# Turning the normalised x of one batch by DMA transpose instead of on TensorE, in a fused linear-attention and MLP kernel

## The chip, the cores and the metric

The kernel runs on one core of a Trainium2 chip. The metric is the time of one execution on the device, in microseconds; lower is better. A time is given as the median of several executions, and one more execution was recorded with a profile.

## The reference, cut to what matters

There are 8 batches, 8 heads, 576 positions and 64 numbers per head. Attention has no softmax: one 64x64 matrix per head is formed from k and v, and q is multiplied by it.

```
kv  = einsum('bhsd,bhse->bhde', k, v)
o   = einsum('bhsd,bhde->bhse', q, kv)
x   = o / sqrt(mean(o*o over the 64 of a head) + 1e-6) * g_norm   # heads joined: [8, 576, 512]
xn  = (x - mean(x)) / sqrt(var(x) + 1e-6) * g_ln                  # over the 512
out = x + relu(xn @ w_ch1) @ w_ch2                                # 512 -> 2048 -> 512
```

## The kernel before, in words

**Tiles.** The 576 positions of a batch are four tiles of 128 rows and a remainder of 64. Remainders of two batches make one tile, so a ninth block, "rem", has four tiles. Every tile of rows passes through these steps (class `Tile`):

- `o` (L259): four small matmuls on TensorE of the turned q (`qt`) with the batch's `kv_pack`, into PSUM `o_ps`.
- `sq` (L265, ScalarE), `red` (L286, VectorE), `root` (L296, ScalarE), `inv` (L303), `y` (L291), `x` (L310) and `xc` (L320), all on VectorE: the two normalisations, without the last division. `xc` ends in a bf16 tile [128 rows, 512].
- `var` (L328, ScalarE): the row variance, used only at the very end of the tile.
- `turn`: `xc` must be laid with its 512 along the partitions before the first big matmul. With `turn(True)` TensorE transposes the four 128x128 blocks into the PSUM tile `tp` (L336) and ScalarE copies `tp` into the columns of this tile in `xT_blk` (L338). With `turn(False)` one DMA transpose issued by SyncE (SP) does it (L340).

**Big matmuls.** `mm1` (L401) multiplies `w1_sb` by columns of `xT_blk` and ScalarE applies relu into `m` (L404). `mm2` (L417) multiplies `m` by `w2_sb`; `finish` adds x on VectorE into `o_sb` (L422) and SP issues two stores to `out` (L435, L436).

**The order of the work** is written by hand. The main program only calls `mm1` and `mm2` of one block after another, and `tick()` ahead of each group of `mm1` and ahead of each four steps of `mm2`. A tick is a slot; before the matmuls of slot n are issued, everything that `at(n, ...)` has put on the agenda for n is issued. Batch b has the slots 32b to 32b+31. Batch 1 has `mm1` in 32 to 47 and `mm2` in 48 to 63. Batch 2 runs `mm1(2, 0, 2)`, which reads the columns of tiles 0 and 1, in 64 to 71; `mm1(2, 2, 2)`, which reads those of tiles 2 and 3, in 72 to 79; and `mm2` in 80 to 95. From batch 3 on, `mm1` takes all four tiles at once.

`plan_tile(s, make, turn_at, on_pe)` puts `o`, `sq`, `red` of a tile at slot s, `y`, `x`, `xc` at s+2, `var` at s+6 and `turn(on_pe)` at `turn_at`. Each engine does its instructions strictly in the order issued, so a slot is also a place in the queue of every engine.

**Around the change.** q of batch 2 is turned by DMA, planned at slot 36.5 (`turn_q_dma`, copy L201 on VectorE, DMA transpose L203 on SP). The remainder tile of batches 0 and 1 is at slot 62, turned by DMA at 69. Batch 3 has `kv_of(3)` (L234) at 55, `turn_q_dma(3)` at 56.7 and its tiles at 65, 70, 75, 80, turned by DMA six slots later. GpSimd issues the loads of k, v and q of batch b (L93, L94) once a one-element copy, `gate` (L98), has read the last piece of the turned q of batch b-1. Batches 0 and 1 are turned on TensorE, batches 3 to 7 and "rem" by DMA.

Buffers: two PSUM banks for `o_ps`, one ("misc") shared by `tp` and `kv_ps`, three for `mm1` (`p1`), two for `mm2`; four `xc` tiles, freed when their turn is done; three `xT_blk`.

Of the kernel before, what the change touches and what calls it, by code (L numbers as in the profile page):

```python
# [14 lines left out]
def kernel(  # L15
# [183 lines left out]
    def turn_q_dma(b):  # L199
        q_p = kv_in.tile([128, JJ, H, D], bf16, tag="qp", bufs=2)  # L200
        nc.vector.tensor_copy(q_p.rearrange("p j h d -> p h j d"), q_in[b % NB])  # L201
        q_t = qt_pool.tile([128, JJ, HP, 128], bf16, tag="qt", name="qt")
        nc.sync.dma_start_transpose(  # L203
            q_t.rearrange("p j hp t -> p (j hp) t"), q_p.rearrange("p j h d -> p (j h d)"))
        qts[b] = q_t
# [34 lines left out]
    def new_block(n, bufs):  # L240
        x_blk = xpool.tile([128, 4, Dm], f32, tag=f"x{n}", bufs=bufs, name="x_blk")
        st_blk = xpool.tile([128, 3, 4], f32, tag=f"st{n}", bufs=bufs, name="st_blk")
        xT_blk = xpool.tile([128, nK, 512], bf16, tag=f"xT{n}", bufs=bufs, name="xT_blk")
        return x_blk, st_blk, xT_blk
# [98 lines left out]
    def main_tile(b, j, pool=None, tag="ops"):  # L343
        q_t, kvp = qts[b], held[b]
        if b not in blks:
            blks[b] = new_block("main", 3)
        return Tile([(slice(0, 128), lambda hp: q_t[:, j, hp, :], kvp)], blks[b], j, pool, tag)

    def rem_tile(b):
        mms = []  # L350
        for half, bb in enumerate((b - 1, b)):
            qt, kp = qts.pop(bb), held.pop(bb)
            mms.append((slice(half * 64, (half + 1) * 64),
                        lambda hp, qt=qt: qt[:, J, hp, :64], kp))
        if "rem" not in blks:
            blks["rem"] = new_block("rem", 1)
        return Tile(mms, blks["rem"], b // 2)

    def plan_tile(s, make, turn_at, on_pe):
        box = []  # L360

        def first():
            t = make()
            box.append(t)
            t.o()
            t.sq()
            t.red()

        def second():
            t = box[0]  # L370
            t.y()
            t.x()
            t.xc()

        def third():
            box[0].var()

        def fourth():
            box[0].turn(on_pe)

        at(s, first)
        at(s + 2, second)
        at(s + 6, third)
        at(turn_at, fourth)
# [72 lines left out]
    def at(slot, fn):  # L457
        agenda.setdefault(int(slot), []).append((slot, fn))
# [145 lines left out]

    at(36, lambda: kv_of(2))
    at(36.5, lambda: turn_q_dma(2))
    for j, s, tn in ((0, 46, 53), (1, 51, 58), (2, 55, 63), (3, 59, 68)):
        plan_tile(s, lambda j=j: main_tile(2, j), tn, True)
    plan_tile(62, lambda: rem_tile(1), 69, False)
    at(78, lambda: rstd_of(2))  # L610

    for b in range(3, B):
        s = 32 * b
# [69 lines left out]
```

## Time and profile before

| | |
|---|---|
| median of 3 runs | 294.49 us (293.52 to 294.82) |
| the profiled execution, own time | 294.47 us |
| its span in the profile | 292.7 us |
| TensorE matmul busy | 281.8 us, 96% of the span |
| ScalarE, VectorE busy | 154.7 us, 150.8 us |
| GpSimd busy | 40.7 us |
| granted TensorE clock | 1.00 |
| moved by DMA | 35.84 MB, mean 122 GB/s |

The profile is of one execution. PE is TensorE's matmul, PEld its weight load, DVE is VectorE, ACT ScalarE, POOL GpSimd, SP SyncE; SPq and POOLq stand for the queues of DMA issues. L340 is line 340 of the kernel. In a line of the timeline the first two numbers are the start and the length in us, and "x4" means that four instructions were merged into it.

### The profile page before, as it was taken

How to read it: one execution, taken by the hardware profiler on the slowest of the kernel's cores; microseconds unless marked ns; L12 is line 12 of the kernel's file. 1: busy time of each engine (PE TensorE's matmuls, PEld its weight loads, DVE VectorE, ACT ScalarE, POOL GpSimd, SP SyncE). 2: the span in 40 equal slices, each digit the busy share in tenths (PEclk: the TensorE clock that was granted, in tenths of full speed). 3: DMA queues.
4: the chain of work that ended last, by engine and by line, in shares of the span. 5: the costliest groups of instructions: out<-in, count | busy, mean ns of one | idle time of the engine just before them, and what ended most of it. 6: DMA issues, size and time to landing. Idle time of an engine off the chain costs nothing.

```text
span 292.7 us, 5775 instructions
## 1 busy us (share of the span) xinstructions
PE 281.8 (96%) x2294; PEld 159.4 (54%) x2320; DVE 150.8 (52%) x335; ACT 154.7 (53%) x341; POOL 40.7 (14%) x68
## 2 busy tenths in 40 slices
PE   8689999999999999999999999999999999999995
PEld 3469855996568744444444444444444444444444
DVE  5677018936896893666266836752677200220022
ACT  3347755885568941892089408930794066017500
POOL 8431610023031002300230014000000000000000
PEclk9999999999999999999999999999999999999999
DMA  7999999559789827993999279939202510131033
GB/s 213 203 204 202 199 204 201 113 94 171 146 150 197 110 57 147 204 175 61 165 183 143 49 155 180 172 57 179 54 18 48 116 36 0 38 74 34 0 74 72
DMA packets 63291, 35.84 MB, mean 122 GB/s; under 512 B 30749, under 2 KB 58269, under 8 KB 63265
## 3 DMA queue, kind: packets, MB, share of 16 engines
q0 software_dynamic: 28016, 17.76, 42.7%
q1 hardware_dynamic: 34736, 16.99, 29.6%
q10 hardware_dynamic: 512, 0.72, 0.7%
q8 instruction: 18, 0.29, 0.4%
q14 instruction: 9, 0.07, 0.1%
HBM read 36.71 MB, written 9.44 MB: 158 GB/s over the span
## 4 chain that ended last, share of the span: by engine, by line
PE 81%; DMA 7%; DVE 5%; ACT 2%; issue 2%; SPq 1%; POOL 0%; POOLq 0%
PE p L401 40%; PE p L417 34%; DMA qt<-q_p 4%; DMA v_in<-in_v_dram 3%; PE o_ps L259 2%; PE kv_ps L234 2%; DVE o_sb L422 1%; DVE ss L286 1%; DMA out_dram<-o_sb 1%; DVE x_blk L310 1%; DVE y L291 1%; ACT m L404 1%; PE tp L183 1%; ACT xT_blk L338 1%; PE p L196 1%
## 5 line engine op out<-in xcount | busy, mean ns | idle before, releaser
L401 PE MATMUL p<-xT_blk,w_sb 128*128 128x128 bf16 (+2 forms) x1018 | 131.7, 285 | 0.8 <-ACT m L404 0.2
L417 PE MATMUL p<-w_sb,m 128*128 128x512 bf16 (+2 forms) x589 | 126.9, 368 | 1.6 <-issue 0.8
L404 ACT ACTIVATE m<-p 128x512 bf16<-128x512 f32 x144 | 85.2, 597 | 45.3 <-PE p L401 43.5
L401 PEld LDWEIGHTS <-w_sb 128*128 128x128 bf16 x1024 | 78.6, 98 | 45.5 <-issue 1.0
L417 PEld LDWEIGHTS <-m 128*128 128x128 bf16 x608 | 56.5, 98 | 60.4
L422 DVE SCALAR_TENSOR_TENSOR o_sb<-p,rstd,x_blk 128x512 f32<-128x512 f32 (+2 forms) x38 | 27.3, 719 | 44.5 <-PE p L417 41.8
L265 ACT ACTIVATE sq<-o_ps 128x512 f32<-128x512 f32 x34 | 20.2, 594 | 39.0 <-PE o_ps L259 38.9
L286 DVE TENSOR_REDUCE ss<-sq 128x8 f32<-128x512 f32 x34 | 23.2, 682 | 19.6 <-ACT sq L265 19.6
L328 ACT ACTIVATE dev<-x_blk,st_blk 128x512 f32<-128x512 f32 x36 | 25.8, 718 | 6.2 <-DVE st_blk L314 6.1
L320 DVE SCALAR_TENSOR_TENSOR xc<-x_blk,st_blk,g_ln_sb 128x512 bf16<-128x512 f32 x34 | 25.5, 751 | 1.2
L291 DVE TENSOR_TENSOR y<-o_ps,inv 128x512 f32<-128x512 f32 x34 | 23.5, 692 | 2.6
L310 DVE SCALAR_TENSOR_TENSOR x_blk<-y,g_norm_sb 128x512 f32<-128x512 f32 x34 | 23.5, 692 | 1.2
L410 DVE RECIPROCAL rstd<-rstd 128x4 f32<-128x4 f32 x9 | 1.6, 174 | 39.3 <-ACT rstd L409 39.3
L303 DVE RECIPROCAL inv<-rms 128x8 f32<-128x8 f32 x36 | 7.2, 200 | 22.5 <-ACT rms L296 22.5
L98 POOL COPY gate<-qt 1x1 bf16<-1x1 bf16 x5 | 0.9, 177 | 116.6 <-DMA qt<-q_p 116.6
L296 ACT ACTIVATE rms<-ss,eps_sb 128x8 f32<-128x8 f32 x36 | 10.8, 299 | 7.7 <-DVE ss L286 6.9
L259 PEld LDWEIGHTS <-qt 128*128 128x128 bf16 (+1 forms) x152 | 9.7, 100 | 8.2 <-DMA qt<-q_p 1.8
L259 PE MATMUL o_ps<-kv_pack,qt 128*128 128x128 bf16 (+1 forms) x152 | 13.3, 221 | 0.3 <-DVE qt L191 0.2
L196 PE MATMUL p<-fill_sb 128*128 128x512 bf16 x27 | 8.7, 483 | 1.4 <-DVE eps_sb L137 1.2
L338 ACT COPY xT_blk<-tp 128x512 bf16<-128x512 bf16 x10 | 5.8, 579 | 2.3 <-PE tp L336 2.3
L328 ACT ACTIVATION_READ_ACCUMULATOR dev<-x_blk,st_blk 128x1 f32 x36 | 6.9, 193 | 0.0
L237 ACT CAST kv_pack<-kv_ps 64x256 bf16<-64x256 f32 x7 | 2.6, 365 | 8.1 <-PE kv_ps L234 8.0
(79 smaller groups left out, 119.4 us busy)
## 6 DMA issues: line engine op xcount, KB each, us to landing
out_dram<-o_sb SPq DMA_DIRECT2D x70, 128.0 KB, 2.4
w_sb<-in_moe_w_ch_dram POOLq DMA_DIRECT2D x8, 512.0 KB, 13.8
k_in<-in_k_dram POOLq DMA_DIRECT2D x7, 320.0 KB, 5.1
v_in<-in_v_dram POOLq DMA_DIRECT2D x7, 320.0 KB, 8.2
q_in<-in_q_dram POOLq DMA_DIRECT2D x7, 320.0 KB, 12.1
q_in<-in_q_dram POOLq DMA_DIRECT2D x8, 256.0 KB, 12.2
k_in<-in_k_dram POOLq DMA_DIRECT2D x7, 256.0 KB, 6.5
v_in<-in_v_dram POOLq DMA_DIRECT2D x7, 256.0 KB, 10.4
```

Source lines behind the costliest of these rows:

```text
L196: nc.tensor.matmul(p1, lhsT=fill_sb[:, :128], rhs=fill_sb, start=True, stop=True)
L259: nc.tensor.matmul(flat[rows, hp * 128:(hp + 1) * 128], lhsT=lhsT_of(hp), rhs=kvp[:, hp, :], start=True, stop=True)
L265: nc.scalar.activation(self.sq_t, self.o_ps, func=AF.Square)
L286: nc.vector.tensor_reduce(self.ss, self.sq_t, axis=AX.X, op=ALU.add)
L291: nc.vector.tensor_mul(self.y_t, self.o_ps, self.inv().to_broadcast([128, H, D]))
L310: nc.vector.scalar_tensor_tensor(x_blk[:, ts].rearrange("p (h d) -> p h d", h=H), in0=self.y_t, scalar=1.0, in1=g_norm_sb.to_broadcast([12 ...
L320: nc.vector.scalar_tensor_tensor(self.xc_t, in0=x_blk[:, self.ts], scalar=st[:, 1, self.ts:self.ts + 1], in1=g_ln_sb, op0=ALU.add, op1=ALU ...
L328: nc.scalar.activation(dev, x_blk[:, ts], func=AF.Square, bias=st[:, 1, ts:ts + 1], accum_out=st[:, 2, ts:ts + 1])
L401: nc.tensor.matmul(p1[:, i, :], lhsT=w1_sb[:, kk, de * 128:(de + 1) * 128], rhs=blk[2][:, kk, sl], start=(kk == 0), stop=(kk == nK - 1))
L404: nc.scalar.activation(m1[:, de0:de0 + per, sl], p1, func=AF.Relu)
L417: nc.tensor.matmul(p2[:, c0:c1], lhsT=m1s[b][:, de, ts * 128:(ts + 1) * 128], rhs=w2_sb[:, de, c0:c1], start=(de == 0), stop=(de == nDe - 1))
L422: nc.vector.scalar_tensor_tensor(o_sb[:, c0:c1], in0=p2[:, c0:c1], scalar=rstds[b][:, ts:ts + 1], in1=blks[b][0][:, ts, c0:c1], op0=ALU.mu ...
```

## The change

Batch 2's four tiles start at slots 44, 48, 52, 57 where they started at 46, 51, 55, 59, and are turned at 50, 54, 59, 64 where they were turned at 53, 58, 63, 68. They are turned by a DMA transpose on SP (L340); the TensorE transposes (L336) and ScalarE copies (L338) of these four tiles are gone. Nothing else is edited.

```diff
     at(36, lambda: kv_of(2))
     at(36.5, lambda: turn_q_dma(2))
-    for j, s, tn in ((0, 46, 53), (1, 51, 58), (2, 55, 63), (3, 59, 68)):
-        plan_tile(s, lambda j=j: main_tile(2, j), tn, True)
+    for j, s, tn in ((0, 44, 50), (1, 48, 54), (2, 52, 59), (3, 57, 64)):
+        plan_tile(s, lambda j=j: main_tile(2, j), tn, False)
     plan_tile(62, lambda: rem_tile(1), 69, False)
     at(78, lambda: rstd_of(2))
```

## The prediction

> **What bounds the kernel now.** I read the page first: the busy table and the chain that ended last.
>
> ```profile
> PE 281.8 (96%) x2294; PEld 159.4 (54%) x2320; DVE 150.8 (52%) x335; ACT 154.7 (53%) x341; POOL 40.7 (14%) x68
> PE 81%; DMA 7%; DVE 5%; ACT 2%; issue 2%; SPq 1%; POOL 0%; POOLq 0%
> ```
>
> The first line alone would not do (a pipelined PE looks busy), but 81% of the chain is PE too, and PE's waits add up to only a few us. So the end is set by what stands in PE's queue: an instruction taken out of it is worth its slot, and a wait put into it costs its length. The question is whether PE will have to wait for the DMA.
>
> Next the timeline of PE where batch 2's tiles are turned, three pieces of it:
>
> ```profile
> 72.69 0.39 PE L336 MATMUL tp<-identity,xc 128*128 128x128 bf16 x4
> 72.91 1.89 PE L417 MATMUL p<-w_sb,m 128*128 128x512 bf16 x8
> ...
> 84.67 1.04 PE L401 MATMUL p<-xT_blk,w_sb 128*128 128x256 bf16 x8
> ...
> 88.39 0.39 PE L336 MATMUL tp<-identity,xc 128*128 128x128 bf16 x4
> 88.61 1.91 PE L401 MATMUL p<-xT_blk,w_sb 128*128 128x256 bf16 x16
> 90.36 0.39 PE L259 MATMUL o_ps<-kv_pack,qt 128*128 128x128 bf16 x4
> 90.58 1.04 PE L401 MATMUL p<-xT_blk,w_sb 128*128 128x256 bf16 x8
> 91.83 3.68 PE L401 MATMUL p<-xT_blk,w_sb 128*128 128x256 bf16 x32 [0.21 <-ACT m L404]
> ```
>
> The reader sees that four transposes occupy PE's queue for 0.22 us (72.69 to 72.91), not the 0.39 shown for them; and gets the slots: 84.67 is slot 64, the first use of tiles 0 and 1; 88.39 is slot 68, 90.36 slot 70, 91.83 slot 71, since eight 256-wide matmuls (0.88 us) make a slot here. Slot 72, the first use of tiles 2 and 3, is 91.83 + 0.88 = 92.71.
>
> Last, what a DMA turn takes: the line of its source over the whole run, then two of its executions alone.
>
> ```profile
> L340 SPq DMA_TRANSPOSE xT_blk<-xc x24: 1189/1236/1427, 88.7 to 229.1; - x24
> DMA to landing us min/median/max: 2.4/3.1/9.3
> ```
>
> ```profile
> DMA to landing us min/median/max: 8.0/8.0/8.0
> ```
>
> ```profile
> DMA to landing us min/median/max: 7.2/7.2/7.2
> ```
>
> SP is held 1.2 us by each issue; the landing spreads from 2.4 to 9.3 us. The 8.0 is the one issued at 88.72, the 7.2 that of 115.39. Asked one by one, those beside no loads take 2.4 to 4.4; those issued after GpSimd has begun a batch's loads take 7.2, 7.3, 7.4, 7.2, 8.0, 8.8 and 9.3. The median of 3.1 is not the price in this stage:
>
> ```profile
> 84.69 0.68 POOL L93 DMA_DIRECT2D k_in<-in_k_dram  x1 [0.34 <-issue]
> ```
>
> The loads of batch 4 begin at 84.69, just when the last of the new turns is due.
>
> **What the Trainium skill says.** "VectorE: DVE Perf Modes", section "The three transpose paths", gives 390 ns for a 128x128 bf16 transpose on TensorE and 1309 ns for the DMA's. The trace shows 219 ns for one and 55 ns of queue each in a row of four, and at best 2.4 us for a DMA of four blocks: same order, other sizes; I use the trace's. "DMA: Bandwidth & Descriptors", section "Queues, rings and completion order", says that each DMA engine goes round-robin, packet by packet, over the queues that have work, and takes each queue in ring order. That agrees with the slow landings beside loads, and means that a turn stands behind the stores that SP issued just before it. "TensorE: Matmul & The Clock Gate", section "Part 1: The HAM clock gate (the "warmup" mystery)", says that an idle window of about 3.4 us halves PE's clock. The trace has no such pause after the start (granted clock 9 in all slices), so no run here shows it; it matters to the slow rival only.
>
> **Removed.** Sixteen transposes in four groups, at slots 53, 58, 63 and 68: 4 x 0.22 = 0.88 us of PE's path, all before slot 72. Four ACT copies (L338, 0.58 us each, about 0.48 from start to start): ACT has room in `mm2`, but the copy at 90.01 stands ahead of the relus that free PSUM for slot 71. Slot 70 ends at 90.58 + 0.88 = 91.46 and slot 71 begins at 91.83: 0.36 us lost on ACT. Without the copy the relu is 0.48 earlier and this goes too. Together 1.24 us; slot 64 comes at 84.67 - 3 x 0.22 = 84.01, slot 72 at 92.71 - 1.24 = 91.47.
>
> **Moved.** The four `o` move ahead, none is added: 0. Tile 0's `o` at slot 44 (64.35) needs q of batch 2, whose DMA transpose begins at 58.76 and lands 5.0 later, 63.76: 0.6 us in hand. VectorE's work is the same. From `inv` to the end of `xc` a tile takes 2.55 us (73.93 to 76.48), `red` 0.6 and `o_sb` 0.66 from start to start. With `o` at 64.4, tile 0's `xc` is ready at about 70.1 (71.8 before). Tile 1's follows at 73.6, tile 2's at 77.8, then the copy for batch 3's q at 78.4 (77.73 before), tile 3's `xc` at 82.6, `red` of the remainder until 83.8. So VectorE waits for PE when the last tile of `mm2(1)` ends at 84.01; before, it was one tile behind and did that `o_sb` only at 85.41.
>
> **Added: four DMA turns in SP's queue**, 1.24 us of issue each. In order:
> - Tile 0, at 70.1. Batch 3's loads are in flight, so up to 9.3 us: 79.4, due 84.01. Hidden by 4.6 us. Behind it in SP stand only the stores of `mm2(1)`, whose `o_sb` is later.
> - Tile 1, behind the first stores, at 75.4. Those loads end at 67.60 + 9.1 = 76.7, so nearer 4.4 than 9.3: 79.8. Hidden.
> - q of batch 3 (3.16 us of issue) at 79.5, after 79.05; it opens the gate for the loads of batch 4, so these begin about 0.4 later, at 85.1. `kv_of(4)` comes at 103.3: nothing.
> - Tile 2, behind it at 82.7, before the loads; due at 91.47. Even 8.7 us would do. Hidden.
> - Stores of the third tile 83.9 to 85.0; of the fourth, with `o_sb` done at 84.9, until 86.1 (0.47 and 0.59 to issue).
> - **Tile 3 at 86.15**, 1.1 us into the loads of batch 4, with 256 KB of stores in front in the same ring. The two nearest cases are that at 115.39 (0.1 us into loads: 7.2) and that at 88.72 (4.0 into them, same stores in front: 8.0). I take 7.6: it lands at 93.75. PE wants it at 91.47 and **waits 2.3 us**. Its cover is gone because 64 is only eight slots from 72 and the slots are 0.9 us.
> - Behind tile 3 stand the turns of the remainder and of batch 3, 1.2 us later; due at slot 96 (115.82). Hidden by far. `xc` has four buffers, each freed by a landing: tile 3's is wanted again by batch 3's tile 2, near 100. Nothing.
>
> Bounds on this wait: from below 0, if tile 3 takes the 4.8 us that the store at 86.18 took (90.95); from above 5.1, if VectorE stays a tile behind (stores done 87.3) and it takes 9.3 (96.6).
>
> **The loads of batch 3 get tile 0's turn beside them.** The second v load lands at 66.27 + 7.5 = 73.8, and `kv_of(3)` takes it at 74.7. A turn alone takes a third of 2 us (DMA share 0.35 in 102 to 104), so v may move by up to 0.7 to 74.5: 0. Bounds: 0 and 0.6.
>
> **Given back.** For batch 4's first tile PE waits for q's DMA: 48 matmuls of 0.2155 from 104.13 end at 114.47, `o` starts at 114.72. A PE that is held at slot 72 lets VectorE and SP catch up, and I take these 0.25 back; without a wait at 72 they stay.
>
> **Sum.** Against the profiled execution's own time of 294.47 (span 292.7 and 1.8 around it; the median of the runs, 294.49, is the same): -0.88 - 0.36 + 2.3 - 0.25 = +0.8, **295.3 us**. That is within 0.5% (1.47 us), about what a measurement of this kernel can tell from no change.
>
> **Rivals.**
> - *The turn is in time.* Tile 3's ring entry gets through before the loads fill the engines, under 5.3 us. For it: loads issued at 84.69 need over 1 us to move anything. Against it: the turn at 115.39, with the same lead, took 7.2. Gain 1.24, 293.2; more than 1.47 if PE gets back some further wait on ACT or q.
> - *A long wait at slot 72: slower.* One mechanism: tile 3 lands after 94.4, 8.3 us after issue; from there the wait exceeds 1.24 + 0.25 + 1.47. At 9.3 it lands at 95.45, PE waits 4.0, and the sum is +2.5: 297.0; a halved clock could follow such a pause and add 1 or 2. For it: 8.8 and 9.3 occur, both with stores in front, and an SP that is a us later does the same. Against: both were issued 5 us into the loads, not 1.
> - *It does not do what it says: slot 64 waits as well*, if the DMA's write into `xT_blk` is ordered against every reader of that tile: 93.75 - 84.01 less the gains, about 303. Against it: ACT's copy into the same columns at 90.01 did not hold the matmuls of 88.61.
>
> **How the numbers follow.** Forecast (wait of 1.2 to 3.0 us) 0.43; in time, or nearly, 0.24, of which 0.10 lies beyond -1.47; long wait 0.30, since SP late and a slow landing both lead there; whole-tile order 0.03. Faster 0.10, same 0.43 + 0.14 = 0.57, slower 0.30 + 0.03 = 0.33. The range, 292.9 to 297.4, reaches from the gain in full with the runs' own scatter of 0.3 to a landing of 9.3 a little late. The forecast's own range is 294.2 to 296.0.
>
> **What would show it.** Right: no L336 after 62.4; on PE one new wait of about 2 us ahead of L401 at 91.5, released by the DMA of `xT_blk`; L340 issued near 86 with a landing of 7 to 8; slot 64 at 84.0. Wrong: no wait at 91.5 (first rival), one over 3 us or a lower granted clock behind it (second), a wait at 84 (third), or a wait at `kv_of(3)` near 74.7.

## The result and the profile after: slower by 1.6%

The changed kernel takes 298.07 us in the median of 6 runs (297.26 to 300.05); the kernel before, run beside it, 293.52 (292.85 to 294.82). The ratio is 1.0157, with a 95% interval of 1.0114 to 1.0199. That is outside the range of the prediction, on its slower side. The profiled execution took 298.17 us, its span is 296.2 us.

The busy table hides it: PE is busy for the same share of a longer span. The table of PE's waits shows it (each line: us in total, times, longest). The kernel before has one line with a DMA in it, the loads of v at the start:

```profile
PE even L219 <- DMA v_in<-in_v_dram: 2.1, 2, 1.3
```

In the changed kernel two are new:

```profile
PE 284.8 (96%) x2304; PEld 159.4 (54%) x2304; DVE 151.3 (51%) x335; ACT 153.4 (52%) x337; POOL 40.7 (14%) x68
...
PE p L401 <- DMA xT_blk<-xc: 3.4, 1, 3.4
...
PE o_ps L259 <- DMA qt<-q_p: 0.4, 1, 0.4
```

The timeline of PE places them:

```profile
83.05 1.04 PE L401 MATMUL p<-xT_blk,w_sb 128*128 128x256 bf16 x8
84.45 0.40 PE L259 MATMUL o_ps<-kv_pack,qt 128*128 128x128 bf16 x4 [0.36 <-DMA qt<-q_p]
84.69 4.53 PE L401 MATMUL p<-xT_blk,w_sb 128*128 128x256 bf16 x40
89.05 0.39 PE L259 MATMUL o_ps<-kv_pack,qt 128*128 128x128 bf16 x4
89.28 1.91 PE L401 MATMUL p<-xT_blk,w_sb 128*128 128x256 bf16 x16
94.59 4.46 PE L401 MATMUL p<-xT_blk,w_sb 128*128 128x256 bf16 x24 [3.41 <-DMA xT_blk<-xc]
98.89 0.39 PE L259 MATMUL o_ps<-kv_pack,qt 128*128 128x128 bf16 x4
```

83.05 is slot 64, 89.05 slot 70, 98.89 slot 75. Sixteen matmuls of 0.11 us end slot 71 at 91.03, and slot 72 begins at 94.59: **3.57 us of nothing**. Then comes what costs nearly half as much again: the 24 matmuls from 94.59 to slot 75 take 4.30 us. Before, the 32 from 91.83 on reached slot 75 in 3.52 us, so 24 took 2.64:

```profile
95.35 0.39 PE L259 MATMUL o_ps<-kv_pack,qt 128*128 128x128 bf16 x4
```

The windows of the changed kernel show why (columns: stretch, length, PE busy, granted clock as a share of full speed, DMA share, GB/s):

```profile
91.00:94.60 3.60, 0.19 (x3) 1.00 1.58 155
94.60:96.00 1.40, 1.40 (x8) 0.60 2.01 38
96.00:97.00 1.00, 1.00 (x7) 0.50 1.28 174
97.00:98.00 1.00, 1.00 (x7) 0.50 1.38 183
98.00:99.00 1.00, 1.00 (x10) 0.86 1.32 188
```

About 0.3 us after PE comes back its clock is at half, and it stays there for 3.4 us. The DMA that PE waited for is the turn of tile 3. SP's timeline up to it, and then that one execution alone ("landing" is when the data are there, counted from the start of the issue):

```profile
78.01 0.47 SPq L435 DMA_DIRECT2D out_dram<-o_sb  x1
78.53 0.60 SPq L436 DMA_DIRECT2D out_dram<-o_sb  x1
79.22 3.19 SPq L203 DMA_TRANSPOSE qt<-q_p  x1
82.46 1.28 SPq L340 DMA_TRANSPOSE xT_blk<-xc  x1
83.83 0.53 SPq L435 DMA_DIRECT2D out_dram<-o_sb  x1
84.41 0.60 SPq L436 DMA_DIRECT2D out_dram<-o_sb  x1
85.11 0.54 SPq L435 DMA_DIRECT2D out_dram<-o_sb  x1
85.69 0.61 SPq L436 DMA_DIRECT2D out_dram<-o_sb  x1
```

```profile
L340 SPq DMA_TRANSPOSE xT_blk<-xc x1: 1346/1346/1346, 86.3 to 86.3; - x1
...
DMA to landing us min/median/max: 8.2/8.2/8.2
```

From 78.01 on SP issues one thing after another with no gap over 0.1 us, and reaches tile 3 at 86.34. 86.34 + 8.2 = 94.54: PE starts 0.05 later.

**The sum of the trace.** The two profiled executions differ by 3.5 us in span, but PE of the changed one was 0.95 ahead before anything was changed (slot 44 at 63.40 instead of 64.35; its waits on the first loads of v are 1.0 us in all, not 2.1). So 4.45 are to be explained, and the medians differ by 4.55. Slots 44 to 64 took 19.65 instead of 20.32: -0.67, the three groups of transposes. From slot 64 to the end of slot 71: 7.98 instead of 8.04, -0.06. The pause: +3.57. The half clock: 4.30 - 2.64 = +1.66. That is 4.50. From slot 75 to the end the two take the same time within 0.04 us.

### The profile page after: what moved, and what is told of

It is laid out like the page before. It is cut to its first block, busy times and chain, and to the rows that moved or that the text cites. A ratio compares the mean times of both kernels' runs of the same rounds, so it can differ in the third digit from the quotient of the medians.

```text
span 296.2 us, 5775 instructions
## 1 busy us (share of the span) xinstructions
PE 284.8 (96%) x2304; PEld 159.4 (54%) x2304; DVE 151.3 (51%) x335; ACT 153.4 (52%) x337; POOL 40.7 (14%) x68
## 4 chain that ended last, share of the span: by engine, by line
PE 83%; DMA 6%; DVE 5%; ACT 2%; issue 1%; POOL 1%; SPq 0%; DVEq 0%; POOLq 0%
PE p L401 39%; PE p L417 37%; DMA xT_blk<-xc 3%; DMA q_in<-in_q_dram 2%; PE o_ps L259 2%; PE kv_ps L234 2%; DMA out_dram<-o_sb 1%; DVE y L291 1%; DVE o_sb L422 1%; DVE ss L286 1%; DVE x_blk L310 1%; PE tp L183 1%; PE p L196 1%; ACT m L404 0%; ACT sq L265 0%
## 5 line engine op out<-in xcount | busy, mean ns | idle before, releaser
L401 PE MATMUL p<-xT_blk,w_sb 128*128 128x128 bf16 (+2 forms) x1024 | 133.5, 288 | 3.7 <-DMA xT_blk<-xc 3.4
L417 PE MATMUL p<-w_sb,m 128*128 128x512 bf16 (+2 forms) x608 | 129.7, 368 | 0.0
L404 ACT ACTIVATE m<-p 128x512 bf16<-128x512 f32 x144 | 85.4, 596 | 51.3 <-PE p L401 49.3
L401 PEld LDWEIGHTS <-w_sb 128*128 128x128 bf16 x1024 | 79.5, 99 | 49.5 <-DMA xT_blk<-xc 3.7
L234 PEld LDWEIGHTS <-k_in 128*64 128x64 bf16 x280 | 5.4, 112 | 2.6 <-issue 2.5
```

The source lines that it names most:

```text
L401: nc.tensor.matmul(p1[:, i, :], lhsT=w1_sb[:, kk, de * 128:(de + 1) * 128], rhs=blk[2][:, kk, sl], start=(kk == 0), stop=(kk == nK - 1))
L404: nc.scalar.activation(m1[:, de0:de0 + per, sl], p1, func=AF.Relu)
L417: nc.tensor.matmul(p2[:, c0:c1], lhsT=m1s[b][:, de, ts * 128:(ts + 1) * 128], rhs=w2_sb[:, de, c0:c1], start=(de == 0), stop=(de == nDe - 1))
```

## The experiments

Theory: the whole loss is tile 3's landing, which the loads of batch 4 slow down, and the half clock that the pause sets off. Rivals: the other three DMA turns cost as much; the earlier slots cost; SP is simply late, loads or not; the clock has another cause. The kernel before took 293.2 to 293.3 us beside these runs.

### Tile 3 back on TensorE

```diff
-        plan_tile(s, lambda j=j: main_tile(2, j), tn, False)
+        plan_tile(s, lambda j=j: main_tile(2, j), tn, j == 3)
```

> The changed kernel with tile 3 of batch 2 alone turned by TensorE again (at slot 64); tiles 0 to 2 stay on the DMA, all slots as changed. Theory (the whole loss comes from tile 3's landing: a wait of 3.6 us at slot 72 and the half clock of some 3.4 us that follows it, 1.7): no wait of L401 on the DMA of xT_blk, granted clock 1.00 throughout, about 293.0 to 293.6 us, 0.998 to 1.000 of before. Rival (the other three DMA turns cost as much, by their traffic or their place in SP's queue): stays above 295. Rival (the low clock has nothing to do with the wait): clock still falls somewhere in batch 2, about 295.

Measured: 292.32 us, ratio 0.9962 (0.9948 to 0.9977); clock 1.00; no wait on `xT_blk`. The loss is gone with one of four DMA turns, and with the other three in place the kernel is faster than before. The time came out 0.7 us below the lower end of what I had expected.

### The slots alone, and the DMA alone

```diff
# the slots alone (changed slots, all four on TensorE)
-        plan_tile(s, lambda j=j: main_tile(2, j), tn, False)
+        plan_tile(s, lambda j=j: main_tile(2, j), tn, True)
# the DMA alone (slots of before)
-    for j, s, tn in ((0, 44, 50), (1, 48, 54), (2, 52, 59), (3, 57, 64)):
+    for j, s, tn in ((0, 46, 53), (1, 51, 58), (2, 55, 63), (3, 59, 68)):
```

> The slots alone: the changed slots with all four tiles turned by TensorE as before. Theory (the move of the slots costs only a wait of some 0.4 us on batch 3's q, and takes the relu wait of 0.36 us ahead of slot 71 away or not): 0.998 to 1.001 of before, no wait on a DMA of xT_blk, clock 1.00. Rival (the earlier slots are what costs): 295 or more.

> The DMA turns alone: batch 2's four tiles at the slots of before (46, 51, 55, 59, turned at 53, 58, 63, 68), but by DMA. Theory: tile 3 is issued behind the same stores of mm2(1), which in the kernel before end at 87.3 us, so near 87.4, into the loads; it lands after 7.2 to 8.8 us, near 95.5; slot 72 comes near 91.7; a wait of 3.5 to 4.5 us and the halved clock behind it: 297.5 to 299.5 us, like the changed kernel or a little worse. Rival (starting the tiles sooner is what costs): under 295.

The slots alone: 293.14 us, 0.9993 (0.9984 to 1.0003), no difference. In its trace two things cancel. The pause of 0.36 us ahead of slot 71 is gone, but slot 64 comes 20.68 us after slot 44 instead of 20.32, since two of the four groups of transposes now wait for their `xc`.

The DMA alone: 299.94 us in the median of 4 runs (297.03 to 301.69), 1.0190 (1.0150 to 1.0231). The profiled execution is the fastest of the four. PE waits in it for 0.34 us at slot 64, for tile 1, and at slot 72 as in the changed kernel:

```profile
93.91 4.21 PE L401 MATMUL p<-xT_blk,w_sb 128*128 128x256 bf16 x24 [3.18 <-DMA xT_blk<-xc]
```

The window ahead of it has the clock at 0.81 in the mean:

```profile
92.50:94.00 1.50, 0.09 (x1) 0.81 1.40 192
```

It is at half from 93.4 to 96.9, so it fell about 0.5 us before PE had work again. The other three runs have mean clocks of 0.989, 0.989 and 0.983 where this one has 0.993; no trace shows where they lost the rest.

So the move to the DMA is what costs, not the sooner start. Tile 3 was issued 22.8 us after slot 44 here and 22.9 us in the changed kernel: with its turn planned four slots earlier it came out of SP no sooner. In both traces SP issues one thing after another up to then, from 76.03 here and from 78.01 there, so what is ahead of it in SP's queue sets the time.

### The loads of batch 4 held until tile 3 has landed

```diff
-           lambda b=b: load_batch(b, qts[b - 1][:1, J, HP - 1, 127:]))
+           lambda b=b: load_batch(b, blks[2][2][:1, nK - 1, 511:] if b == 4 else
+                                  qts[b - 1][:1, J, HP - 1, 127:]))
```

> The changed kernel with the loads of batch 4 gated on the last columns of batch 2's xT_blk instead of on batch 3's turned q, so that they begin only when tile 3's turn has landed; nothing else moves, tile 3 is issued at the same place in SP's queue behind the same stores. Theory (the loads beside it make the landing slow): tile 3 issued near 86, landing in 2.5 to 4.4 us, by 90.5 and before slot 72; no wait, clock 1.00, about 293 us. Rival (SP issues it too late, or the stores in front in its ring hold it, loads or not): landing still near 8 us, wait over 3 us, 297 to 298.

Measured: 292.44 us, 0.9971 (0.9961 to 0.9980). Tile 3 is issued at 85.92, behind the same four stores:

```profile
L340 SPq DMA_TRANSPOSE xT_blk<-xc x1: 1304/1304/1304, 85.9 to 85.9; - x1
...
DMA to landing us min/median/max: 2.5/2.5/2.5
```

2.5 us instead of 8.2, with nothing changed but the loads beside it. That settles the cause of the slow landing: neither the issue time nor the stores in front of it made it slow without the loads. Whether the stores add to it when the loads are there was not tried.

### Tile 3 sooner in SP's queue

```diff
-    for j, s, tn in ((0, 44, 50), (1, 48, 54), (2, 52, 59), (3, 57, 64)):
+    for j, s, tn in ((0, 44, 50), (1, 48, 54), (2, 52, 59), (3, 57, 59.6)):   # or (3, 57, 62)
```

> The changed kernel with tile 3's turn planned at slot 59.6 instead of 64, which puts it in SP's queue right behind tile 2's and ahead of the four stores of mm2(1)'s last two tiles. Theory: issued near 83.8 us instead of 86.3, lands in 2.5 to 4.4 us, before the loads of batch 4 move anything; no wait at slot 72, clock 1.00; what is left is the gain of 0.9 us of transposes and up to 0.4 of a wait on ScalarE, less 0.4 for a new wait on batch 3's q at slot 65: 0.997 to 0.999 of before, 292.6 to 293.3 us. Rival (traffic of the loads reaches it anyway): landing 7 us or more, about 91, wait under 0.5, 294.

> The changed kernel with tile 3's turn planned at slot 62 instead of 64: behind the stores of mm2(1)'s third tile, ahead of those of the fourth. Issued near 85.1 us, as the loads of batch 4 are issued. Theory: landing of about 7.2 us, 92.3, a wait of 1 to 1.5 us at slot 72, too short to halve the clock: clock 1.00, about 294 us, 1.001 to 1.003 of before. Rival (any wait of PE here halves the clock): clock falls to 0.5 behind the wait and the time is near 296. Rival (the stores in front were what held it): landing under 5 us, no wait, 293.

At 59.6: 292.61 us, 0.9984 (0.9973 to 0.9994). At 62: 292.59 us, 0.9977 (0.9968 to 0.9986); here I had expected a wait of 1 us and there was none. The landings, at 59.6 and then at 62:

```profile
DMA to landing us min/median/max: 2.4/2.4/2.4
```

```profile
DMA to landing us min/median/max: 5.9/5.9/5.9
```

The first was issued 1.1 us ahead of the first load of batch 4 (85.4 against 86.47), the second at the same moment (84.57 and 84.58); in the changed kernel it was 1.3 us after (86.34 and 85.04) and took 8.2. So 2.4 us in SP's queue decide nearly 6 us of landing. My 7.2 for the middle case was too high: it lands at 90.5, when slot 72 begins. The profiled execution of the kernel with 59.6 is the slowest of its 22 runs, 294.46; what it lost lies at the start of the kernel, as told below.

### Filling the pause

The changed kernel, with matmuls of zeros ahead of the one that waits. Their results are never read.

```diff
     at(78, lambda: rstd_of(2))
+    at(72, lambda: fill(8))       # or fill(14)
```

> The changed kernel with eight matmuls of zeros (128x512, 1.7 us of TensorE, results never read) put ahead of the first matmul of slot 72, so that the wait for tile 3 comes after work instead of after nothing; nothing else changes. Theory (the pause of 3.6 us halves the clock for some 3.4 us): tile 3 lands at the same time, the pause shrinks to about 1.8 us, clock stays 1.00, and the kernel with more work is FASTER than the changed one by about 1.7 us: 296 to 296.8. Rival (the low clock is not caused by the length of the pause): clock falls all the same, time unchanged at 298.

Eight: 298.42 us, 1.0175 (1.0146 to 1.0203), so the time did not fall as expected. Two of its four runs still had a mean clock of 0.994; the traced one, the fastest at 297.40, has 0.999. The changed kernel, unedited, was then run beside a longer filling:

> The changed kernel once more, unedited, on the same chip as the next one, since its runs scatter from 297.3 to 300.1 and by clock (mean 0.994 in some, 0.989 in others) where the kernel before scatters by 0.3 us. Theory (the scatter is that of tile 3's landing and of how many half-clock windows the pause sets off): median 297.5 to 298.5, mean clock 0.994 or lower in every run. Rival (the first measurement was of a disturbed chip): under 296.

> The changed kernel with fourteen matmuls of zeros (3.0 us, results never read) put ahead of slot 72, where eight gave a mixed answer: in the profiled run the clock stayed at 1.00 and the first 24 matmuls behind the wait took 2.6 us where the changed kernel needs 4.3, but two of four runs still showed a mean clock of 0.994 and the median did not fall. Theory (those two had landings so late that 1.7 us of filling did not cover the pause): with 3.0 us the clock stays at 0.997 or more in nearly all runs, the pause is 0.5 to 1.5 us, and the time is 1 to 1.7 us below the changed kernel's on the same chip, near 296.5. Rival (filling delays what it covers, or the clock falls whatever stands there): no faster than the changed kernel beside it.

The changed kernel again: 298.33 us, 1.0176 (1.0157 to 1.0195), mean clock 0.993 or 0.994 in all five runs. With fourteen: 297.86 us, 1.0156 (1.0135 to 1.0177), mean clock 0.997 to 0.999 in all four. The group behind the wait, in the changed kernel again, with eight and with fourteen:

```profile
94.65 4.46 PE L401 MATMUL p<-xT_blk,w_sb 128*128 128x256 bf16 x24 [3.53 <-DMA xT_blk<-xc]
```

```profile
94.83 2.79 PE L401 MATMUL p<-xT_blk,w_sb 128*128 128x256 bf16 x24 [2.35 <-DMA xT_blk<-xc]
```

```profile
94.88 2.79 PE L401 MATMUL p<-xT_blk,w_sb 128*128 128x256 bf16 x24 [1.19 <-DMA xT_blk<-xc]
```

With PE kept at work the same 24 matmuls take 1.67 us less, behind the same DMA: **the pause does halve the clock here**. But the median fell by 0.5, not 1.7, and the two intervals overlap. The trace shows where the rest went. Tile 3 landed later: from slot 64 to the end of the wait it is 12.35 us (82.53 to 94.88) instead of 11.67 (82.98 to 94.65), a loss of 0.68. And 0.7 was given back 110 us further on, at the first tile of batch 7, where PE now arrives ahead of q:

```profile
206.35 0.40 PE L259 MATMUL o_ps<-kv_pack,qt 128*128 128x128 bf16 x4 [0.54 <-DMA qt<-q_p]
```

From the end of `kv_of(7)` to this point it is 11.08 us, and 10.37 in the changed kernel. 1.67 - 0.68 - 0.71 leaves 0.3. Why the landing was slower in both filled kernels (8.8 and 9.0, against 8.2 and 8.3) stays open.

The length of one pause is not all that counts. In the traces of the two kernels with tile 3 at 59.6 there is no wait at slot 72, and yet the clock is at half once for 3.4 us, near the start: from 18.0 us in one, where the only recorded wait of PE in the 5 us before is 0.84, and from 10.7 in the other (the last experiment), after waits of 1.71 and 0.74. The clock in the first of them, 0.79 in the mean from 14 to 21 us:

```profile
14.00:21.00 7.00, 5.85 (x67) 0.79 1.24 206
```

What sets it off there stays open.

### The wait on batch 3's q

With tile 3 sooner in the queue PE still waits 0.3 to 0.4 us at slot 65, for batch 3's q. Here batch 3's first tile starts a slot later, in the kernels with tile 3 at 62 and at 59.6.

```diff
             o = s + d + (10 if b == 3 else 12) + 5 * j
+            o += b == 3 and j == 0          # slot 66 instead of 65
```

> The kernel with tile 3 turned at slot 62, and batch 3's first tile at slot 66 instead of 65 (its later steps a slot later too), so that TensorE reaches it after batch 3's q has landed. Theory: the wait of 0.37 us on that q, and the weight loads held by it, go: 0.3 to 0.5 us less than with slot 65, 292.1 to 292.3, 0.996 to 0.997 of before. Rival (the wait only moves, to the next q of batch 4 or to tile 3's landing, due 0.1 us after it): tile 3's landing appears as a wait of about 0.3 us and the time stays at 292.6.

> Tile 3 turned at 59.6 and batch 3's first tile at slot 66: with the turn at 62, moving that tile only turned the wait on batch 3's q into one on tile 3's landing (0.42 us). Theory: tile 3 lands two us before slot 72, so neither wait is left; 0.3 to 0.5 us below the kernel with 59.6 alone: 292.1 to 292.3, 0.996 to 0.9975 of before. Rival (the wait moves on to the next thing, batch 4's q at its first tile): no wait near slots 65 and 72, one of about 0.4 us near 113 us, time 292.6.

With tile 3 at 62 the rival was right: 292.64 us, 0.9981 (0.9970 to 0.9993), and the wait moved to tile 3:

```profile
90.55 2.78 PE L401 MATMUL p<-xT_blk,w_sb 128*128 128x256 bf16 x24 [0.42 <-DMA xT_blk<-xc]
```

With tile 3 at 59.6 nothing is late: **292.07 us, 0.9965 (0.9955 to 0.9976)**, and from 60 to 100 us its table of PE's waits is empty. It beats both kernels. Its traced execution, 293.81, is the slowest of 22 and has the half clock at 10.7 us.

## Why the prediction was wrong

The direction of the sum was right (+0.8 forecast) and so was its place. Its size was not: in PE's own time, counted from slot 44, it is +4.45. The step that failed is the wait at slot 72. It was put at 2.3 us and measured 3.57, and with the longer pause came the half clock of 1.66 us, which the forecast had left out. Without that, 298.07 would be about 296.4 by this sum (an estimate), inside the range.

- **Removed, 1.24 us: right.** From slot 44 to slot 75 the kernel without any wait takes 29.71 us, the kernel before 31.00; the medians differ by 1.19 (293.26 to 292.07). The pause of 0.36 us ahead of slot 71 is gone with the slots alone, too.
- **Tiles 0, 1 and 2 hidden: right.** Their landings were 9.0, 4.2 and 2.5 us, and slot 64 began on time (19.65 us after slot 44, 19.66 forecast). `kv_of(3)` did not wait.
- **Tile 3's issue, 21.8 us after slot 44: wrong, it was 22.9.** VectorE's steps came out a little longer than forecast (tile 0's `xc` to tile 1's 3.68 us, not 3.5; tile 1's to tile 2's 4.33, not 4.2; in each stands a wait of 0.37 on `rms`), so the copy for batch 3's q came 0.45 later against PE and its DMA 0.67 later; and the two pairs of stores ahead of tile 3 held SP for 1.28 and 1.23 us, not 1.06 each.
- **Landing of 7.6: wrong, 8.2.** The cause that the prediction named, loads of batch 4 beside it, is shown by holding them back. The other thing that it named, the stores in front, does not slow the turn by itself: 2.5 us behind the same four stores, 2.4 behind none of them.
- **Slot 72 at 7.46 us after slot 64: wrong, 7.98.** Between them stands the first tile of batch 3, for whose q PE stood still 0.52 us (0.36 of it recorded as the wait). I had used that landing for the gate of the loads and not asked who on PE waits for it.
- Together these make the wait: 2.3 + 1.1 + 0.6 - 0.5 = 3.5, measured 3.57.
- **The half clock, 1.66 us: left out of the forecast.** I had it only as an addition to the slow rival, since "TensorE: Matmul & The Clock Gate", section "Part 1: The HAM clock gate (the "warmup" mystery)", in the Trainium skill puts the idle window at 3.4 us and I forecast 2.3. A wait whose cost jumps beyond some length was priced as if the cost grew evenly, so an error of 1.3 us in the wait became one of 2.9. The page agrees with these runs in kind and in the 3.4 us that the half clock lasts. It does not agree in the length of the pause: in the kernel with the DMA alone the clock fell within a recorded pause of 3.18 us, and near the start of two others after none over 1.71, while 2.35 us in the kernel with eight fillings did not set it off.
- **Given back, 0.25: wrong, nothing.** From the tile at slot 75 to the end the two kernels take 197.35 and 197.31 us.

So the mechanism up to the wait was that of the forecast, and the outcome that of the slow rival: it had the threshold at a landing of 8.3 us, and the landing was 8.2 with a later issue. The rival had also named the half clock, at 1 or 2 us. The base of 294.47 was about 1 us high, since the kernel before took 293.2 to 293.5 in the longer series. On that base the forecast would have been 294.0 to 294.3 and the miss larger.

Two of the six runs of the changed kernel, 299.50 and 300.05, have a mean clock of 0.989 instead of 0.993 or 0.994. A second window at half clock would give that, such as the one near the start that two traces show; no trace of those two runs was taken, so this is not shown.

## What to carry to other kernels

A DMA turn in the place of one on the busiest engine is worth the engine's time only if its landing, at the worst that the same stage shows, is before the use. Look at who issues loads at that moment: here 2.4 us sooner in the issuing queue turned 8.2 us of landing into 2.4, and 1.3 us sooner into 5.9. With the first tile of the next batch a slot later as well, a gain of 0.35% was left where the first placing lost 1.6%. And when the bounds of a forecast wait on TensorE reach the length at which its clock has been seen to fall, give the fall a term in the sum.

## What the runs showed of the hardware

- One 128x512 bf16 DMA transpose landed in 2.5 us when GpSimd's batch of loads was held back, and in 2.4 us when it was issued 1.1 us ahead of the first load. Issued together with the first load it took 5.9 us (7.2 for one in the kernel before, 0.1 us after the first load), and 8.2 to 9.0 us when issued 1.3 us after it.
- After recorded TensorE pauses of 3.41 and 3.53 us the granted clock was 0.50 for 3.4 us; in a pause of 3.18 us it fell 0.5 us before the pause ended. Filling the same pause down to 2.35 or 1.19 us kept it at 1.00 in the traces. Twice near the start it fell after recorded waits of no more than 1.71 and 0.84 us, so the length of one pause does not decide it alone.
- Two DMA transposes of the same shape can hold SP for different times: 1.2 to 1.4 us mostly, but 2.6 us for tile 1's (issued at 74.86 in the changed kernel).
